# Finding the scale of w2 from a sum of squares on ScalarE instead of a largest value on VectorE

## The chip, the cores and the metric

The kernel runs on one core of a Trainium2 chip. The metric is the device time of one execution in microseconds (us); smaller is better. The engines are named as the profile names them: PE is TensorE (matmuls, with PEld its weight loads), DVE is VectorE, ACT is ScalarE, POOL is GpSimd, SP is SyncE, which issues the DMAs of this kernel. Each engine takes its own instructions strictly in the order in which they were issued, and waits for others by semaphores.

## The reference

Two stages follow each other. The first is an attention with a window of 16 positions and, beside it, one summary key and value per block of 32; the second mixes four experts, each of two matrix products with a ReLU between them.

```python
B, H, S, D = 4, 8, 768, 64              # attention
k_sum = k.reshape(B, H, nb, 32, D).max(axis=3)
v_sum = v.reshape(B, H, nb, 32, D).mean(axis=3)
scores = concat(where(|i - j| < 16, q @ k.T / 8, -1e9), q @ k_sum.T / 8 + log(32))
attn   = softmax(scores) @ concat(v, v_sum)

x = attn, as (3072, 512)                # 3072 tokens
p = domain_probs / sum(domain_probs)    # (3072, 4)
for e in range(4):                      # w1[e] is (512, 1024), w2[e] is (1024, 512)
    out += p[:, e] * (relu(x @ w1[e]) @ w2[e])
```

All inputs and the output are float32.

## The kernel before

**Precision.** A float32 product is made from parts. For most of the program a factor is scaled and split into two float16 parts, high and low, and three matmuls (high x high, high x low, low x high) give the product. So that the float16 parts use their range, each expert's w1 and w2 are multiplied by a scale that depends on the size of their entries. That scale is found on the chip.

**Finding the scale.** `scans` is a list of 64 pieces, 16 for each expert in the order of experts 2, 3, 1, 0; a piece is a 128 x 512 block of w1 or of w2, the two alternating. `scan()` loads a piece into one of two buffers of the tag `ws` and calls `largest`, which writes one number per partition into `wmax`. When an expert's 16 pieces are done, `scales_of_weights` reduces `wmax` to `wm` (128 x 2: one column for w1, one for w2), and `scales` takes it across the partitions: a transpose on PE (`pmw`), a maximum (`topw`), a small diagonal (`dgw`) and a matmul with ones, and then a handful of operations on 128 x 2 numbers on DVE (`bigw`, `scalew`), which round the number, invert it and refine the inverse. `one` holds the factor for w1 and the factor that undoes both scales; the factor for w2 is a column of `scalew`.

**Using the scale.** `w1_operands` multiplies two raw blocks of w1 (`wx`) by `one` on ACT and makes seven operands of them (`w1g`), because the expert's products run by a scheme with seven block products in place of eight; casts are on ACT, differences on POOL and DVE. `w2_scaled` and `w2_operands` do the like for w2 (`wr` to `w2s` and `w2g`), with the factor `scale_w[e][1]`.

**Stages.** After a prelude (about 40 us) whose order is written out, the first two groups of 384 tokens run through experts 0 and 1 with the unscaled scheme (names `w`, `ph`, `po`, `hh`, `hl`) while attention for the next tokens goes on beside them. Then come four pairs of token groups. Pair 0 takes experts 2 and 3, which is where scales are used for the first time; its operands of x (`x`, `x_t`, made from `xr`) are made just ahead of it. Pair 1 takes 3, 2, 1, 0, and so on. In these, PE accumulates into banks a, b, c and d (`pha` to `phd` for the first product, `poa` to `pod` for the second), with copies and sums of banks on ACT and DVE between. Attention's pieces (`psc` the scores, `ms` and `rs` the softmax, `aw` the weights, `awT` their transpose by DMA, `px` the values, `xs` the result) are put between the matmuls up to the last pair.

**What sets the order.** No engine's order is written out after the prelude. Every operation is recorded as a `Step` with two estimates, how long it holds its engine and how long until its result may be used (functions `ACT`, `DVE`, `POOL`, `PE`, `SP` of `Step`); `order_of` then plans forwards and backwards ten times with these estimates and with the buffers, and keeps the best order. The positions at which the scans and the pieces of attention enter the recording, and the pace of each stage, are tables of numbers (`KEYS`, `STEPS`, `ENDS`, `SHIFT`, `scan_at`). All recorded operations are issued from one line, so every row of the profile shows L373.

## Time and profile before

| what | value |
|---|---|
| time, median of 3 | 1079.48 us (1079.33 to 1082.24) |
| the profiled execution | 1079.39 us, its span 1077.5 us |
| granted clock of PE, mean | 0.995 |
| busy PE, DVE, ACT, POOL | 98%, 80%, 68%, 56% of the span |
| scans on DVE (`wmax`) | 64 of 673 ns, 42.6 us, from 24.5 to 491.6 us |
| table loads on ACT | 1 of 1283 ns |

The span is the time between the first and the last recorded instruction. The busy share is a union: overlapping instructions count once, so sums of single durations come out higher. A row of the order of time has the start and the duration in us, the engine, the operation, what it writes and reads, and in brackets how long its engine stood idle before it and what ended that. `ACT_TABLE_LOAD` brings a set of functions into ACT; a program has one before the first function that is not in the set that is loaded.

### The profile page before, as it was taken

The page shows a single profiled execution, that of the slowest core. Times are in us where ns is not written, and L with a number is a line of the kernel's source. Part 1 is how long each engine was busy: PE and PEld are TensorE (multiplying, and loading weights), DVE is VectorE, ACT ScalarE, POOL GpSimd, SP SyncE. Part 2 cuts the span into 40 slices and gives each one's busy share as a digit, 9 for nine tenths or more (in the row PEclk, how much of TensorE's full clock was granted, in tenths as well). Part 3 has the DMA queues.
Part 4 walks back from the last instruction along what each step waited for, and adds up shares of the span by engine and source line. Part 5 has one row for each costly group of instructions (what it writes and reads, how often), then busy time and mean ns, then how long its engine had stood idle before and what let it go on. Part 6 is the DMA issues. An engine that isn't in the chain of part 4 may idle for free.

```text
span 1077.5 us, 22082 instructions
## 1 busy us (share of the span) xinstructions
PE 1051.8 (98%) x7497; PEld 707.7 (66%) x7497; DVE 866.0 (80%) x2102; ACT 730.2 (68%) x1992; POOL 607.2 (56%) x716
## 2 busy tenths in 40 slices
PE   9988999899999999999999999999999999999998
PEld 7977888654554555555555568686775567686867
DVE  6898889988877867988988897998767775969473
ACT  5776688887864744976977796988545763748170
POOL 2599588877743211852856887896532352717050
PEclk9999999989999999999999999999999999999999
DMA  8789887987888889789676664657422440424001
GB/s 287 212 202 244 227 220 198 274 270 198 240 245 253 253 232 254 220 268 263 207 231 170 167 176 126 176 163 217 116 83 89 135 149 16 162 66 151 1 15 59
DMA packets 172897, 194.95 MB, mean 181 GB/s; under 512 B 80368, under 2 KB 117232, under 8 KB 172784
## 3 DMA queue, kind: packets, MB, share of 16 engines
q1 hardware_dynamic: 172784, 193.55, 62.3%
q8 instruction: 58, 0.95, 0.4%
q14 instruction: 55, 0.45, 0.1%
HBM read 141.33 MB, written 35.65 MB: 164 GB/s over the span
## 4 chain that ended last, share of the span: by engine, by line
PE 66%; DVE 5%; POOL 2%; ACT 2%; DMA 1%; issue 1%; SPq 0%; DVEq 0%; POOLq 0%; ACTq 0%
PE po L373 16%; PE phb L373 13%; PE pha L373 8%; PE pob L373 7%; PE poa L373 5%; PE phd L373 4%; PE phc L373 4%; PE poc L373 3%; PE pod L373 2%; PE psc L373 2%; PE px L373 1%; POOL w2g L373 1%; DVE wr L373 1%; DMA wr<-in_w2L 1%; ACT ms L373 0%
## 5 line engine op out<-in xcount | busy, mean ns | idle before, releaser
L373 PEld LDWEIGHTS <-w1g 128*128 128x128 f16 x2352 | 229.2, 98 | 174.2 <-issue 13.0
L373 PEld LDWEIGHTS <-h 128*128 128x128 f16 x1764 | 171.0, 98 | 115.9 <-issue 0.5
L373 PE MATMUL po<-w2s,h 128*128 128x512 f16 x1008 | 239.6, 379 | 0.0
L373 PE MATMUL phb<-x_t,w1g 128*128 128x384 f16 x1008 | 195.3, 327 | 4.6 <-DVE phc L373 1.9
L373 POOL TENSOR_TENSOR w2g<-wr,w2g 128x512 f16<-128x512 f32 (+1 forms) x80 | 90.1, 1133 | 114.3 <-ACT w2g L373 112.1
L373 PE MATMUL pha<-x,w1g 128*128 128x384 f16 x672 | 133.3, 329 | 2.9 <-DVE nb L373 2.9
L373 ACT ACTIVATE ms<-ms,nb 96x152 f32<-96x152 f32 x256 | 104.0, 414 | 15.5 <-DVE nb L373 15.2
L373 PEld LDWEIGHTS <-hs 128*128 128x128 f16 x1008 | 98.0, 98 | 12.7 <-issue 0.4
L373 POOL TENSOR_TENSOR v<-qv,v 128x256 f16<-128x256 f32 (+1 forms) x56 | 45.7, 816 | 104.6 <-ACT v L373 89.7
L373 DVE CUSTOM_DVE_ANT_0 ms<-psc,c_sb 96x152 f32<-96x152 f32 x256 | 69.1, 305 | 31.3 <-PE psc L373 30.5
L373 POOL TENSOR_TENSOR h<-r,h 128x384 f16<-128x384 f32 x56 | 57.1, 1025 | 54.1 <-ACT h L373 51.5
L373 ACT CAST w2g<-wr 128x512 f16<-128x512 f32 (+1 forms) x112 | 61.6, 562 | 32.2 <-DVE wr L373 18.7
L373 POOL TENSOR_TENSOR w<-wr,w 128x512 fp32r<-128x512 f32 x48 | 65.3, 1368 | 26.2 <-ACT w L373 20.3
L373 DVE TENSOR_TENSOR aw<-ms,aw 96x512 f16<-96x512 f32 (+1 forms) x104 | 69.7, 686 | 6.3 <-ACT aw L373 6.3
L373 PE MATMUL ph<-xh,w 128*128 128x384 f32 x256 | 69.4, 343 | 5.1 <-ACT w L373 3.6
L373 PE MATMUL phd<-x_t,w1g 128*128 128x384 f16 x336 | 65.6, 326 | 2.6 <-POOL w1g L373 1.7
L373 PE MATMUL phc<-x,w1g 128*128 128x384 f16 x336 | 66.1, 326 | 0.0
L373 PE MATMUL poa<-w2g,h 128*128 128x256 f16 x504 | 65.4, 273 | 0.4 <-DVE nb L373 0.4
L373 PE MATMUL pob<-w2g,hs 128*128 128x256 f16 x504 | 64.0, 273 | 0.3 <-DVE poc L373 0.3
L373 POOL TENSOR_TENSOR ks<-kr,ks 128x304 fp32r<-128x304 f32 x56 | 53.3, 952 | 16.3 <-ACT ks L373 15.7
L373 PE MATMUL po<-w,hh 128*128 128x512 f32 x192 | 60.8, 396 | 0.0
L373 ACT ACTIVATE wr<-wr,scalew 128x512 f32<-128x512 f32 x72 | 51.8, 719 | 11.2 <-DMA wr<-in_w2L 7.7
(195 smaller groups left out, 2350.1 us busy)
## 6 DMA issues: line engine op xcount, KB each, us to landing
wr<-in_w2L SPq DMA_DIRECT2D x112, 256.0 KB, 3.3
w1g<-wdg SPq DMA_DIRECT2D x34, 512.0 KB, 4.1
w1g<-wdg SPq DMA_DIRECT2D x34, 384.0 KB, 3.8
ws<-in_w1L SPq DMA_DIRECT2D x32, 256.0 KB, 3.8
ws<-in_w2L SPq DMA_DIRECT2D x32, 256.0 KB, 3.8
wx<-in_w1L SPq DMA_DIRECT2D x32, 256.0 KB, 4.7
wdg<-w1g SPq DMA_DIRECT2D x16, 512.0 KB, 4.5
wd<-w2s SPq DMA_DIRECT2D x16, 512.0 KB, 5.1
```

Source lines behind the costliest of these rows:

```text
L373: program.append(Step(self.key, lambda: getattr(self.engine, name)(*a, **kw), name, a, kw))
```

## The change

The scan of a w2 piece is now an activation on ACT: each entry is squared (after a factor of 1 + 1/256) in place, and the sum over the 512 columns is accumulated into `wmax`. The scan of a w1 piece is as it was, a maximum on DVE. In `scales_of_weights` the w2 column of `wm` is kept above 2^-120 (DVE), and its square root is taken with a logarithm and an exponential on ACT; the largest of these over the partitions is an upper bound of the largest entry, so the scale is found from it, with a further factor `W2_TOP` of 4, which is put into `one` and taken out of the factor that undoes the scales. The w2 factor is now the third column of `one`. Since the logarithm is not in the set that holds the attention's exponential, the program has a table load before each logarithm and before each exponential that follows it: nine in place of one. The planner's estimate for an activation with an accumulated sum, so far one number, is made to grow with the columns from 200 columns on; it stays 420 ns for attention's 152. The tables of numbers are unchanged. The planner makes a new order from these steps, from about 24 us on.

```diff
@@ Step.ACT
         if op == "activation" and "accum_out" in kw:
-            return 420.0 * (1 + SPARE), 560.0 + 420.0 * SPARE
+            t = 420.0 if n < 200 else 175.0 + 0.85 * n
+            return t * (1 + SPARE), t * (1 + SPARE) + 140.0
@@
-    X_TOP, W1_TOP = 4.0, 0.25
+    X_TOP, W1_TOP, W2_TOP, ROUND = 4.0, 0.25, 4.0, 1.0 + 2.0**-8
@@
     def largest(e, fc, which, raw):
-        V.tensor_reduce(
-            wmax[:, e, which, fc : fc + 1], raw, axis=AX.X, op=ALU.max, apply_absolute_value=True
-        )
+        to = wmax[:, e, which, fc : fc + 1]
+        if which:
+            A.activation(raw, raw, AF.Square, scale=ROUND, accum_out=to)
+        else:
+            V.tensor_reduce(to, raw, axis=AX.X, op=ALU.max, apply_absolute_value=True)
@@ def scales_of_weights(e)
         V.tensor_reduce(m, wmax[:, e], axis=AX.X, op=ALU.max)
+        V.tensor_scalar_max(m[:, 1:2], m[:, 1:2], 2.0**-120)
+        A.activation(m[:, 1:2], m[:, 1:2], AF.Ln)
+        A.activation(m[:, 1:2], m[:, 1:2], AF.Exp, scale=0.5)
         s, back = scales(f"w{e}", m, 2)
-        one = const.tile([P, 2], F32, name=f"one{e}")
+        one = const.tile([P, 3], F32, name=f"one{e}")
+        V.tensor_scalar_mul(one[:, 2:3], s[:, 1:2], W2_TOP)
         V.tensor_scalar_mul(one[:, 0:1], s[:, 0:1], W1_TOP)
         V.scalar_tensor_tensor(
-            one[:, 1:2], back[:, 0:1], 1.0 / (X_TOP * W1_TOP), back[:, 1:2], op0=ALU.mult, op1=ALU.mult
+            one[:, 1:2], back[:, 0:1], 1.0 / (X_TOP * W1_TOP * W2_TOP), back[:, 1:2], op0=ALU.mult, op1=ALU.mult
         )
-        scale_w[e], back_w[e] = (one[:, 0:1], s[:, 1:2]), one[:, 1:2]
+        scale_w[e], back_w[e] = (one[:, 0:1], one[:, 2:3]), one[:, 1:2]
```

## The prediction

> **What bounds the kernel now.** I read the page's engine totals first, then a table of stretches, then the waits and the order of time where PE stands still.

> ```profile
> span 1077.5 us, 22082 instructions
> PE 1051.8 (98%) x7497; PEld 707.7 (66%) x7497; DVE 866.0 (80%) x2102; ACT 730.2 (68%) x1992; POOL 607.2 (56%) x716
> ```

> PE is busy for all but 25.7 us of the span, so what this change can win is idle PE time, and what it can lose is more of it. The table of stretches says where that idle time lies (columns: length, busy us and instructions of PE, PEld, DVE, ACT, POOL, then granted clock):

> ```profile
> 54.00:81.00 27.00, 24.17 (x158) 19.06 (x158) 24.82 (x64) 21.10 (x69) 26.55 (x25) 1.00 0.82 204
> 81.00:108.00 27.00, 23.60 (x191) 19.80 (x191) 22.60 (x51) 16.84 (x51) 26.37 (x31) 1.00 0.99 245
> 162.00:189.00 27.00, 27.00 (x213) 24.12 (x213) 25.34 (x66) 22.89 (x74) 23.59 (x27) 1.00 0.78 195
> 200.00:220.00 20.00, 13.57 (x90) 9.16 (x89) 19.67 (x46) 17.38 (x53) 17.84 (x23) 0.80 0.89 272
> 220.00:240.00 20.00, 19.46 (x129) 11.39 (x128) 16.73 (x44) 17.53 (x49) 12.67 (x17) 0.95 0.85 261
> 240.00:260.00 20.00, 18.12 (x100) 9.37 (x99) 18.39 (x37) 15.97 (x40) 16.24 (x20) 1.00 0.66 174
> 432.00:486.00 54.00, 54.00 (x359) 29.15 (x358) 47.23 (x115) 44.88 (x128) 36.78 (x48) 1.00 0.82 245
> ```

> From 54 to 108 POOL is full (26.55 and 26.37 of 27 us) and PE loses 6.2 us. From 162 to 189 PE is full whatever DVE does, and so it is from 432 to 486. The one deep hole is 200 to 220: PE works 13.57 us, DVE 19.67, and the clock falls to 0.80 and then 0.95, which takes another 0.20 x 13.57 + 0.05 x 19.46 = 3.7 us of PE's rate. Three waits make that hole, and they hang together:

> ```profile
> 200.83 0.15 DVE L373 TENSOR_SCALAR one<-scalew 128x1 f32<-128x1 f32 x1
> 201.46 0.72 ACT L373 ACTIVATE wx<-wx,one 128x512 f32<-128x512 f32 x1
> 208.46 1.12 POOL L373 TENSOR_TENSOR w1g<-wx,w1g 128x256 f16<-128x256 f32 x1
> 209.60 1.27 SPq L373 DMA_TRANSPOSE awT<-aw  x1
> 209.63 0.82 PE L373 MATMUL phd<-x_t,w1g 128*128 128x384 f16 x4 [1.70 <-POOL w1g L373]
> 213.21 0.45 PE L373 MATMUL px<-awT,v 128*64 128x192 f16 x4 [2.76 <-DMA awT<-aw]
> 217.21 3.68 PE L373 MATMUL pha<-x,w1g 128*128 128x384 f16 x11 [1.98 <-DVE nb L373]
> ```

> `one` is expert 2's finished scale. ACT multiplies the first weights by it 0.6 us later, the operand `w1g` made from them is done on POOL at 209.58, and PE and the transpose on SP both start within 0.05 us of that. Then `pha` waits for a full DVE. 1.70 + 2.76 + 1.98 = 6.4 us.

> **The change, its bill.** The rows that price it:

> ```profile
> L373 DVE TENSOR_REDUCE wmax<-ws 128x1 f32<-128x512 f32 x64 | 42.6, 673 | 0.6 <-DMA ws<-in_w2L 0.6
> L373 ACT CAST w<-wr 128x512 fp32r<-128x512 f32 x52 | 31.7, 615 | 2.0 <-DMA wr<-in_w1L 0.9 <-PE po L373 0.7 <-DMA wr<-in_w2L 0.3
> L373 ACT ACTIVATION_READ_ACCUMULATOR ms<-ms,nb 96x1 f32 x224 | 42.4, 189 | 0.0
> L373 ACT COPY sm<-ms 96x96 f32<-96x96 f32 x8 | 2.2, 272 | 0.3
> L373 ACT ACT_TABLE_LOAD x1 | 1.3, 1283 | 0.7 <-PEq L1716 0.7
> L373 DVE TENSOR_SCALAR one<-scalew x4: 141/143/147, 200.8 to 503.6; 128x1 f32<-128x1 f32 x4
> 234.30 0.41 ACT L373 ACTIVATE ms<-ms,nb 96x152 f32<-96x152 f32 x1
> 234.71 0.41 ACT L373 ACTIVATE ms<-ms,nb 96x152 f32<-96x152 f32 x1
> ```

> DVE loses 32 x 0.673 = 21.5 us and gains eight small operations of 0.14, 1.1 us: 866 becomes about 846. A Square over 512 columns with a sum is not in the trace. From above it is a 512-column pass and a read of the accumulator, 0.615 + 0.189 = 0.80 us; from below the same less the 0.19 us by which an exp and its read overlap (they start every 0.41 us, though 0.41 + 0.19 are 0.60), 0.61. I take the middle, 0.70: 22.4 us. Eight Ln and Exp of one column lie between the 0.19 of a read and the 0.27 of a 96-column copy; 0.25 each is 2.0 us. The new program has eight more table loads, 8 x 1.283 = 10.3 us, which the order's planner gives no time. ACT becomes 730 + 35 = 765 us, 71%. Neither total bounds anything; the places do.

> **Term A, expert 2's scale and the hole at 200 to 220.** On DVE before, around `one` (`ms`, `aw` and `rs` belong to attention, `xr` and `x_t` to the operands of x):

> ```order
> L373 TENSOR_TENSOR aw_289<-ms_713,aw_289 96x512
> L373 TENSOR_TENSOR aw_289<-ms_713,aw_289 96x4x24
> L373 TENSOR_SCALAR bigw_613<-bigw_613 128x2
> L373 TENSOR_TENSOR xr_2_596<-xr_2_596 128x192
> L373 TENSOR_REDUCE wmax<-ws_3_720 128x1
> L373 TENSOR_TENSOR scalew_614<-scalew_614,bigw_613 128x2
> L373 TENSOR_REDUCE wmax<-ws_3_740 128x1
> L373 TENSOR_TENSOR xr_2_596<-xr_2_596 128x192
> L373 TENSOR_TENSOR xr_3_598<-xr_3_598 128x192 x2
> L373 TENSOR_SCALAR one_615<-scalew_614 128x1
> ```

> and now:

> ```order
> L374 TENSOR_TENSOR scalew_614<-scalew_614,bigw_613 128x2
> L374 SCALAR_TENSOR_TENSOR hl_0_7_711<-ph_0_7_709,hh_0_7_710 128x384
> L374 TENSOR_SCALAR one_615<-scalew_614 128x1
> L374 TENSOR_SCALAR rs_715<-rs_715 96x4
> L374 TENSOR_TENSOR xr_2_596<-xr_2_596 128x192
> L374 RECIPROCAL rs_715<-rs_715 96x4
> L374 TENSOR_TENSOR xr_2_596<-xr_2_596 128x192
> L374 TENSOR_TENSOR ms_713<-ms_713,rs_715 96x608
> L374 TENSOR_REDUCE wmax<-ws_4_750 128x1
> ```

> The scale now stands ahead of that piece's `ms`, `aw`, `xr` and both reductions. In the trace these were:

> ```profile
> 194.34 1.08 DVE L373 TENSOR_TENSOR ms<-ms,rs 96x608 f32<-96x608 f32 x1
> 196.21 1.21 DVE L373 TENSOR_TENSOR aw<-ms,aw 96x512 f16<-96x512 f32 x2
> 197.68 0.67 DVE L373 TENSOR_REDUCE wmax<-ws 128x1 f32<-128x512 f32 x1
> 198.94 0.69 DVE L373 TENSOR_REDUCE wmax<-ws 128x1 f32<-128x512 f32 x1 [0.29 <-DMA ws<-in_w2L]
> 199.55 1.37 DVE L373 TENSOR_TENSOR xr<-xr 128x192 f32<-128x192 f32 x3
> ```

> 5.0 us together. So `w1g` can be up to 5 us earlier and the first two waits (4.5 us) can go; the third goes only as far as DVE gets through its queue sooner. Against it, DVE stays nearly full there, and ACT takes the w2 scans in the same stretch, 0.70 each. Bounds: 0, and 6.4 + 3.7 = 10.1 us if all three waits and the slow clock go. What is late next is DVE's own queue, so I take less than half: **-4.0**.

> **Term B, expert 3's scale.** Here the chain runs through a busy ACT. Before and now on ACT, the same place (`h` and `w1g` are needed by PE's next matmuls of expert 2, `wm` is the largest value per partition):

> ```order
> L373 ACTIVATE h_2_3_812<-phd_2_1_803 128x384
> L373 ACTIVATE h_2_1_793<-phb_2_0_777 128x384
> L373 CAST w1g_2_795<-wx_4_738 128x256
> L373 ACTIVATE wr_4_845<-wr_4_845,scalew_614 128x512
> L373 CAST w1g_3_831<-wx_6_774 128x256
> ```

> ```order
> L374 ACTIVATE h_2_1_793<-phb_2_0_777 128x384
> L374 ACTIVATE h_2_0_791<-phc_2_0_783 128x384
> L374 ACT_TABLE_LOAD
> L374 ACTIVATE wm_823<-wm_823 128x1
> L374 CAST w1g_2_795<-wx_4_738 128x256
> L374 ACT_TABLE_LOAD
> L374 ACTIVATE wm_823<-wm_823 128x1
> L374 CAST w1g_3_831<-wx_6_774 128x256
> ```

> Two loads and two small activations, 2 x 1.283 + 2 x 0.25 = 3.1 us, now stand in the chain and ahead of `w1g` and `h`. The Ln also waits for DVE's clamp of `wm`, with those casts, POOL's subtractions and PE's `phb` behind it. The chain had little room:

> ```profile
> 234.79 0.16 DVE L373 TENSOR_REDUCE wm<-wmax 128x2 f32<-128x16 f32 x1
> 247.51 1.34 ACT L373 ACTIVATE wx<-wx,one 128x512 f32<-128x512 f32 x2
> 248.27 1.14 PE L373 MATMUL phb<-x_t,w1g 128*128 128x384 f16 x6 [0.46 <-DVE phc L373]
> 250.54 0.81 PE L373 MATMUL pha<-x,w1g 128*128 128x384 f16 x4
> ```

> From `wm` to the first multiplied weights it is 12.7 us, and PE uses them 3 us later, in a stretch where it already waits. Bounds: 0, if the small DVE operations close up, and 5.9 us, the 3.1 with four scans of 0.70 before it. I take **+3.0**.

> **Term C, the other scales.** Expert 1's weights are multiplied and expert 0's as well long before PE asks:

> ```profile
> 431.41 1.32 ACT L373 ACTIVATE wx<-wx,one 128x512 f32<-128x512 f32 x2
> 447.30 1.14 PE L373 MATMUL pha<-x,w1g 128*128 128x384 f16 x6
> 504.23 0.71 ACT L373 ACTIVATE wx<-wx,one 128x512 f32<-128x512 f32 x1
> 512.38 1.14 PE L373 MATMUL pha<-x,w1g 128*128 128x384 f16 x6
> ```

> The cover is about 16 and 8 us, more than the 3.1 added. What can still hurt is a copy out of PE's banks queued behind a load. Six loads outside term B are 7.7 us of ACT, all where PE is full; bounds 0 and 7.7, and since idle ACT time lies beside them (9.1 us from 432 to 486) I take **+1.0**.

> **Term D, 40 to 110 us.** The w2 scans enter ACT's queue among the casts of w:

> ```profile
> PE ph L373 <- ACT w L373: 3.6, 3, 1.6
> ```

> PE waited three times for those casts. One scan ahead of two of the three is **+1.4**; bounds 0 and 6.3 (nine scans).

> Sum: -4.0 + 3.0 + 1.0 + 1.4 = +1.4. The profiled execution took 1079.39 us (span 1077.5 and 1.9 around it; the median shown is 1079.48): **1080.8**.

> **The rivals.** *Faster: the hole closes.* Term A at 8 of its 10.1 us, expert 3's chain absorbed by the small DVE operations, C and D as above: 1079.4 - 8.0 + 2.4 = 1073.8. For it speaks that all three waits trace back to `one` at 200.83 and to a DVE at 98%; against it, that a DVE still over 90% full sets `pha`. It decides from the point where `w1g` is ready before PE reaches `phd`.

> *Slower: ACT takes DVE's place.* From 200 to 260 ACT was busy 17.38 + 17.53 + 15.97 = 50.9 of 60 us. Five scans and two loads with their activations are 3.5 + 3.1 = 6.6 us, which makes 57.5, so the gaps of ACT's dependences no longer fit. Then A gives nothing and B is at its 5.9: 1079.4 + 5.9 + 2.4 = 1087.7. Against it speaks that the planner knows the scans and can move other casts out.

> *Slower: a table load costs twice its row.* If ACT must run empty before each load and fill again, and that takes as long as the load, each costs 2.6 us instead of 1.28; expert 3's chain gets 2.6 us more: 1083.4. The one load of the trace stands at the program's start with nothing before it, so the row can't tell. [...]

> That the change doesn't do what it says is out: 32 scans and nine loads stand in ACT's order.

> **How the numbers follow.** Forecast, no real change, 0.36, its own range 1076.2 to 1082.7; hole closes 0.28; ACT in DVE's place 0.26; dear loads 0.10. A measurement of this kernel tells about 0.3%, 3.2 us, from no change, so faster is 0.28, within 0.36, slower 0.26 + 0.10 = 0.36. The whole range takes in most of both other cases: below, A at its full 10.1 with the +2.4 and some 0.6 of B, 1072.3, taken as 1072; above, 1087.7 with a little more of C, 1089.

> **What would show it.** Step A is right if the three waits near 207 to 217 shrink together and the clock of that stretch rises; wrong if `pha` still waits 2 us or `px` waits for its transpose. Step B is right if the span from `wm` to expert 3's first `wx` grows from 12.7 to about 15.8 us and PE's idle time from 240 to 262 grows by some 3 us. C and D are wrong if PE shows idle time from 378 to 540, or more than 6.2 us from 54 to 108. The scan row on ACT should read 0.61 to 0.80, a table load 1.28. A new order in stretches without scans, after 560, that costs or wins more than 2 us, would make the whole forecast wrong.

## The result

The changed kernel took 1087.78 us (median of 4 runs, 1087.44 to 1087.94), the kernel before 1079.79 us (1079.33 to 1082.24): a ratio of 1.0069, 95% interval 1.0052 to 1.0086. Measured once more beside other runs of before (experiment 5) it was 1.0045, 1.0028 to 1.0061. By these ratios the change costs some 5 to 7.5 us; the first two medians lie 8.0 us apart. One execution of the kernel before, beside experiments 5 to 8, took 2165.89 us and is left out of their ratios. The profiled execution took 1087.79 us with a span of 1085.8, 8.3 us more than the one before.

The page's head and totals, after:

```profile
span 1085.8 us, 22137 instructions
PE 1057.8 (97%) x7497; PEld 709.8 (65%) x7497; DVE 853.3 (79%) x2078; ACT 757.4 (70%) x2072; POOL 608.2 (56%) x716
```

PE has the same 7497 matmuls and is busy 6.0 us longer; its idle time (span less busy) grew by 2.3 us only. Most of that longer time, 4.8 of the 6.0 us, is work at a slow clock, and the table of stretches shows where. Columns as in the prediction: length, busy time of PE, PEld, DVE, ACT and POOL, then PE's granted clock. Before, in cuts that fit both kernels:

```profile
0.00:20.00 20.00, 18.23 (x124) 13.27 (x124) 11.28 (x47) 9.39 (x24) 5.58 (x21) 1.00 0.93 335
...
150.00:178.00 28.00, 27.85 (x188) 23.28 (x187) 24.78 (x72) 23.64 (x72) 25.20 (x28) 1.00 0.89 232
178.00:230.00 52.00, 45.57 (x289) 34.12 (x289) 50.43 (x117) 44.62 (x130) 42.38 (x52) 0.90 0.87 248
230.00:262.00 32.00, 29.58 (x183) 15.98 (x181) 28.06 (x69) 26.80 (x70) 24.46 (x31) 1.00 0.71 203
```

After (the second row is for term D below):

```profile
0.00:20.00 20.00, 17.53 (x103) 12.03 (x104) 9.88 (x39) 8.19 (x21) 3.74 (x16) 0.91 0.90 321
54.00:81.00 27.00, 24.84 (x164) 19.53 (x163) 26.26 (x63) 20.88 (x66) 26.15 (x27) 1.00 0.74 195
81.00:108.00 27.00, 23.15 (x171) 19.06 (x169) 21.12 (x48) 17.16 (x55) 22.22 (x25) 0.87 1.03 242
150.00:178.00 28.00, 25.51 (x171) 20.09 (x171) 22.81 (x75) 24.11 (x70) 22.34 (x28) 1.00 0.83 217
178.00:230.00 52.00, 47.60 (x313) 36.98 (x312) 48.96 (x121) 45.55 (x144) 44.39 (x52) 0.93 0.87 237
230.00:262.00 32.00, 29.85 (x186) 17.15 (x184) 26.20 (x66) 29.54 (x74) 19.95 (x26) 0.95 0.73 213
378.00:540.00 162.00, 160.97 (x1061) 87.67 (x1060) 118.59 (x325) 123.66 (x349) 75.69 (x101) 1.00 0.80 244
```

In each row the loss is PE's idle time (length less busy) and what the slow clock takes (busy x (1 - clock)), as the prediction worked it out for the hole. From such rows, idle + slow clock in us (experiments 5, 1, 9 and 2 are told below; all four have the changed kernel's order, and 5 is the changed kernel itself, in another execution):

| stretch | before | after | 5: after again | 1: no root | 9: no loads | 2: old work |
|---|---|---|---|---|---|---|
| 0 to 20 | 1.8 + 0 | 2.5 + 1.6 | 2.4 + 1.6 | 2.5 + 1.6 | 3.3 + 1.5 | 1.9 + 0 |
| 20 to 81 | 3.1 + 0 | 2.3 + 0 | 2.6 + 0 | 2.3 + 0 | 2.3 + 0 | 2.4 + 0 |
| 81 to 108 | 3.4 + 0 | 3.9 + 3.0 | 4.2 + 3.0 | 4.5 + 2.9 | 4.1 + 3.0 | 4.5 + 2.9 |
| 150 to 178 | 0.1 + 0 | **2.5** + 0 | **2.5** + 0 | 0.2 + 0 | 0.2 + 0 | 0.2 + 0 |
| 178 to 230 | 6.4 + 4.6 | 4.4 + 3.3 | 4.5 + 1.4 | 5.2 + 1.4 | 4.5 + 1.4 | 4.9 + 3.3 |
| 230 to 262 | 2.4 + 0 | **2.1 + 1.5** | **2.2 + 1.5** | 0.6 + 0 | 0.6 + 0 | 0.6 + 0 |
| 378 to 540 | 0.1 + 0 | **1.0** + 0 | **1.0** + 0 | 0.0 + 0 | 0.0 + 0 | 0.0 + 0 |
| all of 0 to 1060 | 22.2 + 4.6 | 24.5 + 9.4 | 24.6 + 7.5 | 20.1 + 5.9 | 19.8 + 5.9 | 19.7 + 6.2 |

The last row stops short of the program's end, where PE runs out of work, and takes in the stretches that are not listed; a clock printed as 1.00 counts as no loss. The sum is 26.8 before and 33.9 after, 7.1 of the span's 8.3 us; the rest is not placed. The bold cells are those that both executions of the changed kernel have and the other three do not; there the change's own loss lies, 6.3 us more than in experiment 1. From 178 to 230 the two executions of the same kernel differ by 1.9 us of slow clock, so a difference of that size there says nothing. PE's rows with the longest new waits, after (start, duration, what it computes, and in brackets the idle time before it and what ended it; `pmw` is the transpose of `wm` and the broadcast that follow it, by which a weight scale is found):

```profile
95.85 0.69 PE L374 MATMUL ph<-xh,w 128*128 128x384 f32 x1 [2.98 <-ACT w L374]
...
164.40 0.27 PE L374 MATMUL pmw<-c_sb,wm 128*2 128x128 f32 x1 [1.67 <-DVE bigx L374]
166.87 0.38 PE L374 MATMUL pmw<-dgw,ones 2*128 2x2 f32 x2 [0.82 <-DVE dgw L374]
...
220.91 0.88 PE L374 MATMUL psc<-ks,qs 64*96 64x152 f32 x10 [1.84 <-POOL ks L374]
240.34 0.27 PE L374 MATMUL pmw<-c_sb,wm 128*2 128x128 f32 x1 [1.71 <-ACT wm L374]
487.00 0.27 PE L374 MATMUL pmw<-c_sb,wm 128*2 128x128 f32 x1 [1.03 <-ACT wm L374]
```

Four of the six stand before `pmw`: experts 2, 3 and 0. The three waits of 6.4 us that made the hole before (`phd`, `px`, `pha`) are gone but for 0.64 us before `pha`; `psc` and others stand there now. The bill itself, as groups of instructions:

```profile
L374 ACT ACTIVATE ws<-ws 128x512 f32<-128x512 f32 x32 | 20.0, 626 | 0.4 <-DMA ws<-in_w2L 0.3
L374 ACT ACT_TABLE_LOAD x9 | 11.5, 1283 | 0.9 <-PEq L1723 0.7
L374 ACT ACTIVATION_READ_ACCUMULATOR ws<-ws 128x1 f32 x32 | 6.1, 191 | 0.0
L374 ACT ACTIVATE wm<-wm 128x1 f32<-128x1 f32 x8 | 1.6, 201 | 0.1
```

### The profile page after: what moved, and what is told of

Its sections match the earlier page's. It is cut to its first block, busy times and chain, and to the rows that moved or that the text cites. A ratio compares the mean times of both kernels' runs of the same rounds, so it can differ in the third digit from the quotient of the medians.

```text
span 1085.8 us, 22137 instructions
## 1 busy us (share of the span) xinstructions
PE 1057.8 (97%) x7497; PEld 709.8 (65%) x7497; DVE 853.3 (79%) x2078; ACT 757.4 (70%) x2072; POOL 608.2 (56%) x716
## 4 chain that ended last, share of the span: by engine, by line
PE 73%; DVE 8%; ACT 5%; POOL 4%; issue 2%; DMA 1%; SPq 0%; DVEq 0%; POOLq 0%; ACTq 0%
PE po L374 20%; PE phb L374 13%; PE pha L374 9%; PE pob L374 6%; PE phd L374 4%; PE poa L374 4%; PE phc L374 4%; PE ph L374 3%; PE psc L374 2%; PE poc L374 2%; PE pod L374 2%; PE px L374 2%; POOL wx L374 1%; DVE aw L374 1%; ACT ms L374 1%
## 5 line engine op out<-in xcount | busy, mean ns | idle before, releaser
L374 PEld LDWEIGHTS <-w1g 128*128 128x128 f16 x2352 | 229.9, 98 | 170.4 <-issue 12.5
L374 PEld LDWEIGHTS <-h 128*128 128x128 f16 x1764 | 171.2, 98 | 116.3 <-issue 0.7
L374 PE MATMUL po<-w2s,h 128*128 128x512 f16 x1008 | 239.6, 379 | 0.0
L374 PE MATMUL phb<-x_t,w1g 128*128 128x384 f16 x1008 | 195.6, 327 | 3.4 <-DVE phc L374 2.6
L374 POOL TENSOR_TENSOR w2g<-wr,w2g 128x512 f16<-128x512 f32 (+1 forms) x80 | 88.2, 1110 | 120.1 <-ACT w2g L374 117.7
L374 PE MATMUL pha<-x,w1g 128*128 128x384 f16 x672 | 133.6, 331 | 0.8 <-DVE nb L374 0.6
L374 ACT ACTIVATE ms<-ms,nb 96x152 f32<-96x152 f32 x256 | 103.8, 413 | 22.9 <-DVE nb L374 22.4
L374 PEld LDWEIGHTS <-hs 128*128 128x128 f16 x1008 | 97.9, 98 | 13.8 <-issue 1.5
L374 DVE CUSTOM_DVE_ANT_0 ms<-psc,c_sb 96x152 f32<-96x152 f32 x256 | 68.2, 305 | 30.6 <-PE psc L374 28.4
L374 ACT CAST w2g<-wr 128x512 f16<-128x512 f32 (+1 forms) x112 | 61.6, 563 | 39.2 <-DVE wr L374 22.6
L374 POOL TENSOR_TENSOR h<-r,h 128x384 f16<-128x384 f32 x56 | 57.3, 1026 | 54.1 <-ACT h L374 51.7
L374 POOL TENSOR_TENSOR v<-qv,v 128x256 f16<-128x256 f32 (+1 forms) x56 | 42.7, 762 | 71.0 <-ACT v L374 71.0
L374 POOL TENSOR_TENSOR w<-wr,w 128x512 fp32r<-128x512 f32 x48 | 67.3, 1410 | 22.7 <-ACT w L374 14.9
L374 PE MATMUL ph<-xh,w 128*128 128x384 f32 x256 | 71.3, 349 | 6.8 <-ACT w L374 3.0
L374 DVE TENSOR_TENSOR aw<-ms,aw 96x512 f16<-96x512 f32 (+1 forms) x104 | 70.9, 705 | 8.0 <-ACT aw L374 7.8
L374 POOL TENSOR_TENSOR qs<-qv,qs 128x192 fp32r<-128x192 f32 x56 | 36.9, 659 | 66.6 <-ACT qs L374 60.2
L374 POOL TENSOR_TENSOR ks<-kr,ks 128x304 fp32r<-128x304 f32 x56 | 55.3, 990 | 25.6 <-ACT ks L374 17.4
L374 PE MATMUL phd<-x_t,w1g 128*128 128x384 f16 x336 | 66.5, 329 | 1.1 <-ACT x_t L374 0.8
L374 PE MATMUL phc<-x,w1g 128*128 128x384 f16 x336 | 66.5, 326 | 0.0
L374 PE MATMUL pob<-w2g,hs 128*128 128x256 f16 x504 | 64.2, 273 | 1.2 <-ACT pob L374 0.9
L374 PE MATMUL poa<-w2g,h 128*128 128x256 f16 x504 | 64.7, 273 | 0.0
L374 PE MATMUL po<-w,hh 128*128 128x512 f32 x192 | 62.8, 400 | 0.5 <-DVE hl L374 0.5
```

What stands on the lines that cost most here:

```text
L374: program.append(Step(self.key, lambda: getattr(self.engine, name)(*a, **kw), name, a, kw))
```

## The experiments

Three theories at the start: the **root** (logarithm, exponential and their table loads), the **scans** (32 passes of 512 columns that ACT has to find room for), and the **order** (the planner's new order by itself). Where an order is kept, each instruction is issued at the place the planner gave it, and only what is issued there is replaced. Ratios are to runs of before on the same chip, with 95% intervals.

| run | median us | before | ratio |
|---|---|---|---|
| 1 changed order, sums of absolute values, no root | 1081.49 | 1080.52 | 1.0004 (0.9992 to 1.0017) |
| 2 changed order, old work | 1081.48 | 1080.52 | 1.0007 (0.9990 to 1.0023) |
| 3 old order, new work | 1095.94 | 1080.52 | 1.0145 (1.0124 to 1.0166) |
| 4 before, order drawn anew | 1082.95 | 1080.52 | 1.0021 (1.0007 to 1.0034) |
| 5 the changed kernel again | 1085.83 | 1080.81 | 1.0045 (1.0028 to 1.0061) |
| 6 as 1, with the loads on an unused column | 1085.33 | 1080.81 | 1.0039 (1.0025 to 1.0052) |
| 7 planner told of the loads | 1089.32 | 1080.81 | 1.0073 (1.0053 to 1.0093) |
| 8 as 1, order drawn anew | 1086.08 | 1080.81 | 1.0038 (1.0020 to 1.0057) |
| 9 as 1, two Relu for Ln and Exp | 1079.61 | 1080.58 | 0.9992 (0.9977 to 1.0006) |
| 10 changed kernel, one pair of loads later | 1085.61 | 1080.58 | 1.0046 (1.0029 to 1.0063) |
| 11 old order, sums of absolute values, no root | 1081.02 | 1080.58 | 1.0003 (0.9992 to 1.0015) |
| 12 as 1, one cast earlier | 1078.29 | 1080.55 | 0.9973 (0.9961 to 0.9984) |

### 1. Without the root

```diff
-            A.activation(raw, raw, AF.Square, scale=ROUND, accum_out=to)
+            A.activation(raw, raw, AF.Abs, accum_out=to)      # W2_TOP 64.0 in place of 4.0
         A.activation(m[:, 1:2], m[:, 1:2], AF.Ln)
+        program[-1].issue = ()                                # keeps its place, issues nothing
         A.activation(m[:, 1:2], m[:, 1:2], AF.Exp, scale=0.5)
+        program[-1].issue = ()
```

> Edit: the changed kernel with every instruction at the place that its planner gave it; ScalarE sums absolute values (Abs) in place of squares, so that no root is needed: the eight Ln and Exp and with them the eight added table loads are gone, and nothing else has moved. Theory 'root' (TensorE's transposes `pmw` stand in its in-order queue and wait for Ln, Exp and two table loads of which the planner knew little or nothing, and each stall is followed by a stretch at half clock): the waits before `pmw` of 1.67, 0.82, 1.71 and 1.03 us shrink to under 0.3 us each, a half-clock stretch or two go with them, and the time falls from 1087.8 to about 1080 (5.2 us of waits and up to 3 us of clock). Theory 'scans' (ScalarE's 26 us of scans delay casts and copies): the scans are all still there, so 1086 to 1088. Theory 'order' (the planner's new order costs the time by itself): 1086 to 1088.

Ratio 1.0004: the loss is gone, with all 32 scans on ACT and every instruction of the other engines at the same place. The stretches that lost time after the change, here:

```profile
150.00:178.00 28.00, 27.81 (x185) 22.42 (x183) 23.76 (x78) 23.18 (x72) 24.93 (x30) 1.00 0.90 232
...
230.00:262.00 32.00, 31.35 (x200) 17.58 (x197) 31.04 (x69) 29.59 (x77) 24.19 (x30) 1.00 0.78 223
378.00:540.00 162.00, 162.00 (x1049) 87.96 (x1048) 120.29 (x325) 118.85 (x337) 81.20 (x107) 1.00 0.83 244
```

PE idles 0.19, 0.65 and 0.00 us where it idled 2.49, 2.15 and 1.03, and no wait before a `pmw` is over 0.2 us. "Root" holds; "scans" and "order" fall.

### 2. The changed kernel's order with the old work

```diff
             A.activation(raw, raw, AF.Square, scale=ROUND, accum_out=to)
+            program[-1].issue = lambda: nc.vector.tensor_reduce(
+                to, raw, axis=AX.X, op=ALU.max, apply_absolute_value=True)
```

with clamp, Ln and Exp issuing nothing and `W2_TOP` 1.0.

> Edit: the planner sees the changed kernel's steps and gives its order, but what is issued at the place of each w2 scan is the old maximum on VectorE, and Ln, Exp, the clamp and the eight table loads are left out. Theory 'order': 1086 to 1088, since only the order is new. Theory 'root': as without the root, about 1080, if VectorE has the 20 us to spare; theory 'scans': about 1080 too, the scans being off ScalarE. If VectorE's load where it is full (98% from 200 to 220 us before) is what set the old hole, 2 to 6 us of it come back: 1082 to 1086.

1.0007, the same as experiment 1. So the order costs nothing, and whether the w2 scans run on DVE or on ACT in it makes no difference that can be measured. The wait of 3 us near 95 us is here too:

```profile
95.10 0.44 PE L374 MATMUL ph<-xh,w 128*128 128x384 f32 x1 [3.01 <-ACT w L374]
```

It comes with the order, not with scans on ACT.

### 3 and 11. The old order with the new work, with and without the root

In 3 the planner sees the steps of before; what is issued differs (shortened):

```diff
         V.tensor_reduce(to, raw, axis=AX.X, op=ALU.max, apply_absolute_value=True)
+        if which:
+            program[-1].issue = lambda: nc.scalar.activation(raw, raw, AF.Square, scale=ROUND, accum_out=to)
...
         V.tensor_reduce(m, wmax[:, e], axis=AX.X, op=ALU.max)
+        program[-1].issue = (program[-1].issue, clamp, Ln, Exp)   # right behind it
```

The factor `W2_TOP` is multiplied into the w2 scale in place, right behind the scale's last step.

> Edit: the planner sees the steps of the kernel before and gives its order, but what is issued at the place of each w2 scan is the Square with its sum on ScalarE, and clamp, Ln and Exp (with their two table loads) stand right behind the maximum `wm`, the scale's extra factor behind the scale. Theory 'order': 1079 to 1081, as before. Theory 'root': the four chains are 3.1 us longer in an order that knows nothing of them, so `pmw` waits up to 3.1 us in TensorE's queue each time: 12 us at most, 1085 to 1092. Theory 'scans': 26 us of scans unplanned on ScalarE, 1085 to 1090; then waits stand before matmuls that need casts of w and h, and not before `pmw`.

Experiment 11 is the same with `AF.Abs`, and without clamp, Ln and Exp.

> Edit: the order of before, the w2 scans as sums of absolute values on ScalarE at the places of the old maxima, no root. It splits the third experiment's 15 us. Theory 'loads': what is left without them is the 32 scans that this order has not planned on ScalarE; if idle time takes them up, 1.000 to 1.003 of before. Theory 'scans': 1.007 to 1.012, with waits before matmuls that need casts of w, w1g or h at 207 to 262 us.

1.0145 with the root, 1.0003 without it. In 3 three of the four scales stop PE:

```profile
240.53 0.37 PE L373 MATMUL pmw<-c_sb,wm 128*2 128x128 f32 x1 [4.45 <-ACT wm L463]
...
426.58 0.27 PE L373 MATMUL pmw<-c_sb,wm 128*2 128x128 f32 x1 [2.16 <-ACT wm L463]
...
507.89 0.27 PE L373 MATMUL pmw<-c_sb,wm 128*2 128x128 f32 x1 [2.33 <-ACT wm L463]
```

Those are 8.9 of the 15 us. Added up as in the table, 0 to 1060 us lose 33.0 + 10.9 in place of 22.2 + 4.6, so much of the rest is slow clock. The time lies above the ranges of all three theories: "root" counted the waits and not the clock behind them. The 32 scans that this order had not planned for ACT cost nothing that can be measured (11).

### 4 and 8. What a new order is worth by itself

4: `SPARE` 0.105 in place of 0.1 in the kernel before.

> Edit: the kernel before, with one margin of its planner's estimates 0.105 in place of 0.1 (every estimated time 0.5% longer), which says nothing of any real duration: the same work in an order drawn anew. Theory 'order' (a new order by itself moves the time by several us): at least 3 us away from 1079.5, to either side. Theories 'root' and 'scans': within 2 us of 1079.5, since the work is the same.

8: experiment 1 without Ln, Exp and clamp in the planner's steps too, so that the order is drawn anew.

> Edit: the changed kernel with sums of absolute values in place of squares, without clamp, Ln and Exp in the planner's steps too, and the order drawn anew: VectorE rid of 32 scans and no root. Theory 'the scans are worth nothing on either engine' (first two experiments): 1078 to 1083, within what a new order does. Theory 'VectorE's relief pays once the root is out of the plan': 1072 to 1076.

1.0021 and 1.0038: 2.4 and 5.3 us slower by the medians. 4 does exactly the work of before, and the work of 8 costs nothing in the kept order (1). For 4 the theories had said under 2 us or at least 3, from 1079.5: it is 3.4 from that number, but 2.4 from the runs of before beside it, which lies between. 8 came out above both its ranges (1072 to 1076 and 1078 to 1083). With 1 and 2, whose order cost nothing, a new order by itself has moved this kernel by 0 to 5 us. Differences of that size between kernels that were each planned anew say nothing on their work.

### 5 and 6. The loads without the dependence

5 is the changed kernel, unchanged, beside the next three.

> Edit: none; the changed kernel once more, on the chip and beside the runs of before that the next three share. Every theory: 1.006 to 1.008 of the time before, 7 to 8 us. If its share of before is under 1.004 here, the first measurement had caught it on a bad chip, and what was read from it falls.

1.0045, under the 1.006 to 1.008 that was expected and above the 1.004 below which the first measurement would have fallen. Its profile has the same waits in the bold cells of the table.

In 6, Ln and Exp work on a column that nobody reads; `wm` has sums of absolute values and needs neither:

```diff
         A.activation(m[:, 1:2], m[:, 1:2], AF.Ln)
+        program[-1].issue = lambda: nc.scalar.activation(root, root, AF.Ln)
         A.activation(m[:, 1:2], m[:, 1:2], AF.Exp, scale=0.5)
+        program[-1].issue = lambda: nc.scalar.activation(root, root, AF.Exp, scale=0.5)
```

> Edit: as in the first experiment (changed kernel's order, sums of absolute values, no root), but ScalarE still runs each Ln and Exp at its place, with the eight added table loads, on a column that nobody reads and that waits for nobody. So ScalarE does all the work of the change, and only the dependence of `pmw` on it is gone. Theory 'TensorE waits in its own queue' (the loss is the `pmw` transposes standing in TensorE's queue until Exp is done): 1080 to 1082, waits before `pmw` under 0.3 us. Theory 'ScalarE is held up' (the loss is the casts, copies and h behind the loads): 1086 to 1088, with the waits before matmuls that need h, w or w1g.

My theory at this point, that `pmw` waits in PE's queue for Exp, expected 1080 to 1082 us. It took 1085.33, which is not to be told from 5; the other theory had 1086 to 1088. Rows of DVE and PE show why:

```profile
159.59 0.17 DVE L374 TENSOR_SCALAR rs<-rs 96x4 f32<-96x4 f32 x1 [2.90 <-ACT ms L374]
...
165.99 0.27 PE L374 MATMUL pmw<-c_sb,wm 128*2 128x128 f32 x1 [1.96 <-DVE bigx L374]
...
244.52 1.14 PE L374 MATMUL phb<-x_t,w1g 128*128 128x384 f16 x6 [1.60 <-ACT phb L374]
```

Expert 2's `pmw` waits as long as with the root in its chain. At expert 3 the wait before `pmw` is gone (expert 0's too), and a copy out of PE's banks behind the loads (`phb`) holds PE for 1.60 us instead. The expert 2 chain reads off the changed kernel's own trace. ACT first, then DVE:

```profile
153.35 1.28 ACT L374 ACT_TABLE_LOAD   x1
154.64 0.20 ACT L374 ACTIVATE wm<-wm 128x1 f32<-128x1 f32 x1
154.86 1.28 ACT L374 ACT_TABLE_LOAD   x1
156.16 0.42 ACT L374 ACTIVATE ms<-ms,nb 96x152 f32<-96x152 f32 x1
...
157.39 0.19 ACT L374 ACTIVATE wm<-wm 128x1 f32<-128x1 f32 x1
```

```profile
155.22 0.14 DVE L374 TENSOR_TENSOR bigx<-bigx 128x1 f32<-128x1 f32 x1
158.01 0.17 DVE L374 TENSOR_SCALAR rs<-rs 96x4 f32<-96x4 f32 x1 [2.65 <-ACT ms L374]
...
163.91 0.34 DVE L374 SCALAR_TENSOR_TENSOR xs<-px,xs 128x192 f32<-128x192 f32 x1
164.17 0.14 DVE L374 TENSOR_SCALAR bigx<-bigx 128x1 f32<-128x1 f32 x1
```

Exp was done at 157.58, and `pmw` started at 164.40, so it did not wait for Exp. Two loads stand ahead of attention's exps `ms`; DVE needs their sums for `rs` and stands idle for 2.65 us; all that is behind it in DVE's queue is late, and `pmw` starts 0.09 us after the `bigx` that the trace names as its releaser. Which of the instructions there (`bigx`, or the copies `xs` out of PE's banks right beside it) PE needs was not separated.

### 9. The steps without the loads

```diff
+        program[-1].issue = lambda: nc.scalar.activation(m[:, 1:2], m[:, 1:2], AF.Relu)   # at Ln's place
+        program[-1].issue = lambda: nc.scalar.activation(m[:, 1:2], m[:, 1:2], AF.Relu)   # at Exp's place
```

> Edit: the changed kernel's order, sums of absolute values, and at the places of Ln and Exp two Relu of the same column, which need no table load. The chain from VectorE's maximum over ScalarE to `pmw` has its two extra steps and their waits; only the eight loads are gone (ScalarE 10.3 us shorter). Theory 'loads' (each pair of loads makes ScalarE 2.6 us late, for `pmw` or for whatever stands behind it): 1.000 to 1.002 of the time before, no wait before `pmw` over 0.4 us. Theory 'steps' (one more engine in the chain is what costs): 1.004 to 1.006, and `pmw` of expert 3 still waits over 1 us.

0.9992. The chain over ACT is back in full, only the eight loads are missing (in these stretches ACT is busy 23.34 and 29.94 us, and 23.18 and 29.59 in experiment 1, so neither has a pair of loads):

```profile
150.00:178.00 28.00, 27.82 (x186) 22.59 (x184) 23.97 (x78) 23.34 (x75) 24.87 (x31) 1.00 0.87 231
...
230.00:262.00 32.00, 31.44 (x209) 17.91 (x206) 29.92 (x69) 29.94 (x81) 23.79 (x30) 1.00 0.80 233
```

With 6, which keeps the loads and drops the dependence, this settles it: what costs are the table loads, not the longer chain. A pair, two loads of 1.28 us, makes ACT 2.6 us late, and whichever engine's queue needed ACT next paid: 2.49 us of PE's time before `pmw` in the changed kernel, 1.60 before `phb` in 6.

### 10. One pair four exps later

Expert 2's Ln and Exp are held back until ACT has issued the four exps `ms`; ACT's queue, otherwise as it was:

```diff
+ACTIVATE ms x4
 ACT_TABLE_LOAD
 ACTIVATE wm
 ACT_TABLE_LOAD
-ACTIVATE ms x3
 ACTIVATE wm
-ACTIVATE ms
```

> Edit: the changed kernel with all its work; of its order one thing is moved: expert 2's Ln and Exp with their two loads stand behind the four exps `ms` that stood between and behind them on ScalarE, 1.2 us later. In the sixth experiment VectorE waited 2.90 us for those exps, with a copy out of one of TensorE's banks behind it in its queue, and `pmw` waited 1.96 + 0.78 us though nothing of it depended on Exp. If that chain is right, the two waits of 1.67 and 0.82 us before expert 2's `pmw` shrink to under 0.8 us together, while expert 3's 1.71 and expert 0's 1.03 stay: about 2 us of the 5 to 7, 1.002 to 1.004 of before. If expert 2's `pmw` waits for Exp itself, a later Exp makes its wait longer or leaves it: 1.004 to 1.007.

The time did not follow: 1.0046, as in 5. The two waits before expert 2's `pmw` went from 2.49 to 0.96 + 0.80 = 1.76 us, not below 0.8. DVE no longer waits for `ms`, but now for a later cast on ACT:

```profile
163.72 2.19 DVE L374 TENSOR_TENSOR aw<-ms,aw 96x512 f16<-96x512 f32 x2 [1.89 <-ACT aw L374]
```

So the exps were the first to be late, not the only ones; moving the pair moves the wait along ACT's queue. A gain of 0.7 us is below what these runs can show.

### 7. The planner told of the loads

```diff
+        if op == "activation" and n == 1:
+            return 1500.0, 1600.0
```

> Edit: the changed kernel, with the planner's time for an activation of one column raised from some 100 to 1500 ns (1283 of the table load and 200 of the activation), and the order drawn anew. Theory 'TensorE waits in its own queue': the planner now puts `pmw` behind other matmuls until Exp is done, 2 to 4 of the 5.2 us of waits go and some clock with them: 1081 to 1084. Theory 'ScalarE is held up': the work is the same, 1085 to 1089. A new order by itself moves the time by up to 3 us to either side (the fourth experiment's 2.3).

1.0073, against 1.0045 for the untold planner beside it, a little above both ranges. The planner did what was asked: the largest wait before a `pmw` is 0.52 us. But the order is another, with new waits such as

```profile
264.50 2.10 PE L376 MATMUL po<-w2s,h 128*128 128x512 f16 x7 [2.50 <-DVE w2s L376]
```

and its idle time from 0 to 1060 us is 25.5 us, against 24.5 untold; 6.9 of it lies behind 540 us, where untold 4.1 do. A truer estimate was worth less here than what a new order moves. "Unplanned" was thus not shown to be the reason why the loads cost.

### 12. A version that beats both

The kernels in the changed order (after, 1, 2, 9) lose some 4 us of idle time and 3 of slow clock from 81 to 108 us, most of it at the cast that ended the 3 us wait. In experiment 1's kernel that cast is moved in ACT's queue, and its remainder in POOL's:

```diff
 ACT:  ACTIVATE xs                 POOL: TENSOR_TENSOR w (of the w2 block)
+ACT:  CAST w (w1 block 3)        +POOL: TENSOR_TENSOR w (w1 block 3)
 ACT:  CAST aw x2                  POOL: TENSOR_TENSOR qv, ks, xl
 ACT:  ... CAST v
-ACT:  CAST w (w1 block 3)        -POOL: TENSOR_TENSOR w (w1 block 3)
```

> Edit: the first experiment's kernel (the changed kernel's order, sums of absolute values, no root) with one load's two parts moved: ScalarE's cast of that w1 block stands ahead of the two casts `aw`, about 2.4 us earlier, and POOL's remainder of the same block ahead of `qv`, `ks` and `xl`. All runs in this order had PE wait 2.96 to 3.01 us at 92 to 97 us for that cast and then 0.7 to 1.1 us for POOL, followed by 6.8 us at half clock. Theory 'idle and slow clock add up to the time': 2 to 3 us of the waits go, and if the half-clock stretch goes with them another 3 us: 0.995 to 0.998 of the time before, which would beat both kernels. Theory 'the next wait takes over' (the DMA of that block lands at about 93 us, and the delayed casts are needed next): 0.999 to 1.001.

0.9973 (0.9961 to 0.9984): 3 us faster than before, the only kernel here that is. In its profile the waits at that place are 0.98 and 0.73 in place of 2.98 and 1.11:

```profile
95.81 0.44 PE L374 MATMUL ph<-xh,w 128*128 128x384 f32 x1 [0.98 <-ACT w L374]
97.17 0.61 PE L374 MATMUL ph<-xh,w 128*128 128x384 f32 x2 [0.73 <-POOL w L374]
```

with two new ones of 0.63 and 0.65 behind them: 1.1 us net. The slow stretch at 98 us is still there, and between 20 and 81 us the profile has another, which takes 1.8 us and which experiment 1's has not. So the rest of the gain is not shown by this profile, whose execution, at 1080.76 us, is the slowest of the twelve that were timed.

## Why the prediction was right or wrong

The forecast, no real change at 1080.8 us, did not come: the kernel is slower, by more than the forecast's own range reached (1082.7), and inside the whole range. The slower side had 0.36.

**Term A (-4.0; mechanism half right).** The hole shrank: from 178 to 230 us 6.4 + 4.6 us became 4.4 + 3.3, so -3.3, and -5.1 in the profile of experiment 5. But not because DVE lost its scans: with them back on DVE in the same order (experiment 2) it is 4.9 + 3.3. The new order did it, and not by an earlier scale. In the time of the span `one` is no earlier (203.11, before 200.83); PE comes to its first `phd` 12.9 us behind `one` where it came 6.6 us behind it, with other matmuls between, and finds the operands there. Before, then after:

```profile
207.44 0.50 PE L373 MATMUL phd<-x_t,w1g 128*128 128x384 f16 x2
```

```profile
203.11 0.14 DVE L374 TENSOR_SCALAR one<-scalew 128x1 f32<-128x1 f32 x1
216.04 0.34 PE L374 MATMUL phd<-x_t,w1g 128*128 128x384 f16 x1
```

That a relief of a 98% full DVE shortens the hole was what the prediction leaned on; experiments 1 and 2 differ by nothing that the whole time shows.

**Term B (+3.0; size right, place wrong).** From `wm` to the first multiplied weights of expert 3 it is 17.0 us (235.85 to 252.88) in place of 12.7, 4.3 more where 3.1 was expected. But PE's idle time from 230 to 262 us did not grow (2.4 before, 2.1 after; from 240 to 262, the stretch that the prediction had named, 1.9 and 0.8). The prediction followed the chain to `wx`, where the weights are multiplied; PE meets it earlier, at `pmw`, which stands in its own queue ahead of matmuls that need nothing of it. It waited there 1.71 us, and 1.5 us of slow clock followed: 3.2 us, near the 3.0 by luck of two errors.

**Term C (+1.0) is the step that failed.** "Six loads outside term B are 7.7 us of ACT, all where PE is full" is wrong for expert 2's pair at 153 to 156 us. The prediction had read that PE from 162 to 189 is full "whatever DVE does", from a trace in which DVE was never late there. After the change DVE came 2.65 us late, and PE lost 2.49 us from 162.7 to 166.9. The covers named for experts 1 and 0 reached from `wx` to `pha` and again left out `pmw`; expert 1's pair cost nothing, expert 0's 1.03 us, in the stretch from 378 to 540 where idle PE time was to count against the step. Term C measured 3.5 us of idle time, 3.3 more than in experiment 1.

**Term D (+1.4).** PE's idle time from 54 to 108 us stayed (6.2 before, 6.0 after), so the test that was set did not fail, but the clock fell to 0.87 from 81 to 108, 3.0 us. It is in experiments 1, 2 and 9 as well, so it belongs to the new order, not to w2 scans among the casts.

**What the sum lacked.** It counted slow clock only for the hole of term A. After the change the slow clock takes 9.4 us in place of 4.6, and that is two thirds of the loss that the stretches show; in the profile of experiment 5, the same kernel, it takes 7.5. 1.6 of it, from 0 to 20 us, is no effect of the change: some profiles have it and others do not (experiments 1 and 9 have it, 2 has not; of the kernels without loads in other orders, 4 and 11 have it, before has not). 3.0 of it, from 81 to 108 us, is the new order's. What both profiles of the changed kernel have beyond experiments 1 and 9 is the 1.5 us at expert 3.

**The bill** was right: scans on ACT 0.626 us, 0.61 to 0.84 from their start to that of what follows without a gap, mostly 0.62 (0.70 taken), table loads 1.283, Ln and Exp 0.20 (0.25). ACT's busy time rose by 27.2 us, 35 predicted, and DVE's fell by 12.7, 20 predicted; the single durations add up to 38 us more and 18 less, and busy time counts overlaps once.

**The rivals.** "ACT takes DVE's place" gave 1087.7, the measured time, and is wrong all the same: in it the hole stays as it was (measured: 3.3 us less) and expert 3 pays 5.9 us (measured: 3.2), and ACT with all its scans and no loads is not slower (experiments 1, 9, 11). A time that fits is not a mechanism. "A table load costs twice its row" falls on the rows themselves (expert 3, after):

```profile
236.46 0.50 ACT L374 ACTIVATE h<-phc 128x384 f16<-128x384 f32 x1
236.98 1.28 ACT L374 ACT_TABLE_LOAD   x1
238.27 0.20 ACT L374 ACTIVATE wm<-wm 128x1 f32<-128x1 f32 x1
238.38 0.39 ACT L374 CAST w1g<-wx 128x256 f16<-128x256 f32 x1
238.79 1.28 ACT L374 ACT_TABLE_LOAD   x1
240.08 0.20 ACT L374 ACTIVATE wm<-wm 128x1 f32<-128x1 f32 x1
```

The load starts 0.02 us after the end of what is before it, and what follows starts 0.01 us after the load; the `h` ahead of it takes 0.50 us, as elsewhere (mean 0.48). The cost is 1.28 and the tenth of a microsecond by which neighbours on ACT otherwise overlap (0.09 for the first `wm` and the `w1g` behind it). "The hole closes" came true in idle time at its three waits, and others took their place.

## What to carry to other kernels

Price a table load by what stands behind it in ACT's queue and then in the queues of the engines that need those results: 10 us of loads cost 5 to 7.5 us here although ACT was idle for 30% of the time, while 26 us of scans cost nothing. Where a bound on a maximum is all that is wanted, take one from functions that the loaded set has (sums of absolute values in place of sums of squares with a root: 1.0004 of before in experiment 1, 1.0045 and 1.0069 with the root in the same order). Compare planned kernels with their orders kept: a redrawn order alone moved this one by up to 5 us, and one cast moved by hand in a kept order, with its remainder, was worth 3.
